# Attention and experts in one kernel: mark steps split, small planes moved between engines, block 0's queries turned by DMA, new issue sequences

## The chip, the cores and the metric

The kernel runs on one core of a Trainium2 chip. The metric is the device time of one execution in microseconds; of the kernel before there are three, 710.06, 710.90 and 711.39 us. TensorE (PE) does matmuls, VectorE (DVE) and ScalarE (ACT) read PSUM and SBUF, GpSimd (POOL) reads only what others have put into SBUF, and SyncE (SP) issues nearly all DMAs.

## The reference

For each of 4 batches, a key/value image of 384 x 32 x 128 is averaged over 4 x 4 windows to 768 rows and multiplied by `w_sr`; the result is both keys and values of an attention over 12288 queries of width 128. Its 49152 output rows go through a mixture of 8 experts: the gate's largest logit names one expert, whose two layers (128 to 1024 with a ReLU, 1024 to 128) are applied and scaled by the gate's probability.

```python
kv_flat = kv.reshape(B, H//4, 4, W//4, 4, C).mean(axis=(2, 4)).reshape(B, -1, C) @ w_sr
a = softmax(q @ kv_flat.T / sqrt(C));  x = a @ kv_flat          # B x 12288 x 128
e = argmax(x @ w_gate);  g = softmax(x @ w_gate)[e]
out = g * (relu(x @ w1[e]) @ w2[e])                             # per token
```

## The kernel before

**Tiles and stages.** The 49152 queries are cut into 96 blocks of 512, 24 to a batch. `keys(b)` loads and pools a batch's keys (12 loads of 512 KB; for batch 0 the last four come as 8 halves), multiplies them by `w_sr` and makes from them the scaled keys KT, the values v16 and the square M. `expert(b)` guesses the expert that the batch's tokens will choose from the mean value (`guess`, L837), loads that expert's `raw` weights, and sorts and packs its 1024 hidden units into 384 places (the side on which each unit lies, L945; keys, classes, the permutation PU, L1052; w1U and w2U). `block(t)` then does one block: queries in halves of fp16 turned to qT; scores s by two matmuls for each of three pairs of key tiles; ACT's exponential e; DVE's difference r (L1285); po from r, qT, v16 and M; halves xp of po, turned to x; three hidden tiles ph on w1U; and py on L and w2U, scaled to y and stored.

**Marks.** Tokens whose expert is not the guessed one, or that are not sure, are marked in `code`; `marks` (L1470) does so for 24 blocks at a time, for the last batch in two parts. Its steps go to and fro between DVE and POOL. One of them, `quiet` (L1518), needs flags that PE sums (`seen`, L1512) when all hidden tiles of those blocks are done. Lists of marked tokens are then counted (L1536 or L1543, L1810 to 1813), and a loop at the end (L1855) redoes what is listed.

**The order of the work.** Every operation is declared by `op(engine, duration, function, time, needs, gives, buffers)`. ORDER holds for each engine the sequence in which its operations are issued; a number is an operation's place among those that the code declares for that engine. WAYS names the choices that are taken where an operation is declared in two ways (`way=(name, 0 or 1)`): with the name in WAYS the second holds, without it the first. Names are for example `q3` for the cast of block 3, `l5` for reading block 5's logits by DVE (else ACT), `x7` for splitting block 7's po by ACT and POOL (else ACT and DVE). The engines issue in order: an instruction that waits holds up all behind it on its engine, and SP's DMAs likewise. A planner with durations merges the sequences; it puts filler matmuls (`fill`, L1846) on PE where its own time line has a hole before 110 us or after 690 us. After a DVE operation with `lock=True` it makes the next POOL instruction wait for that one.

**Turning queries.** For `t < TURNED` (L1250, blocks 0 and 1) PE transposes the f32 queries, ACT copies them to fp16 and DVE subtracts (L1259). For the others POOL casts (L1263) and subtracts (L1265), and SP issues a transposing DMA (L1267).

## Time and profile before

| | us |
|---|---|
| three runs | 710.06, 710.90, 711.39 |
| the profiled execution | 711.34 |
| its span, first to last instruction | 709.5 |
| PE, DVE, ACT, POOL busy in it | 687.5, 623.9, 606.5, 533.3 |
| TensorE's granted clock, mean | 0.998 |

A busy share is an average over the span. The start (keys and the first expert) and the end have other limits than the 80 or so blocks between, and are looked at by themselves in the rows below. In a row of a timeline the first two numbers are start and duration in us, `[1.2 <-X]` is idle time before it and what ended it, and `x3` a count.

### The profile page before, as it was taken

The numbers are of one execution on the slowest core, as the hardware profiler recorded it, in microseconds if no ns is written. First come the engines' busy times: TensorE is split into PE (matmuls) and PEld (weight loads), VectorE is DVE, ScalarE is ACT, GpSimd is POOL, SyncE is SP. The second block draws the span as 40 slices with busy tenths as digits, with TensorE's granted clock in tenths as the row PEclk, the third lists the DMA queues.
The fourth block names the chain that finished last, engine by engine and source line by source line (L and its number), as shares of the span: only waits on it lengthen the run. The fifth ranks groups of instructions, "written<-read, shape, count | busy, mean of one in ns | idle before, by whom it ended". The sixth has DMA issues, their size and how long they took to land.

```text
span 709.5 us, 20719 instructions
## 1 busy us (share of the span) xinstructions
PE 687.5 (97%) x7853; PEld 542.0 (76%) x7853; DVE 623.9 (88%) x1279; ACT 606.5 (85%) x1128; POOL 533.3 (75%) x768
## 2 busy tenths in 40 slices
...
GB/s 334 216 252 131 234 260 196 150 214 202 207 238 239 220 236 201 178 205 200 202 221 223 247 226 262 124 206 221 178 204 108 200 126 184 234 150 124 164 67 101
DMA packets 325253, 139.84 MB, mean 197 GB/s; under 512 B 210668, under 2 KB 316270, under 8 KB 325152
## 3 DMA queue, kind: packets, MB, share of 16 engines
...
HBM read 60.69 MB, written 26.90 MB: 123 GB/s over the span
## 4 chain that ended last, share of the span: by engine, by line
PE 75%; DVE 9%; ACT 6%; DMA 5%; issue 3%; POOL 2%; SPq 0%; ACTq 0%; POOLq 0%; DVEq 0%
PE b L487 32%; PE po L487 23%; PE s L487 18%; DVE r L1285 4%; ACT e L1282 3%; DMA x<-xp 2%; DMA qT<-qp 2%; DVE xp L1326 1%; DMA kv<-in_kv_dram 1%; DVE y L1426 1%; ACT g L1391 1%; ACT b L1391 1%; ACT xp L1325 1%; POOL g L1387 0%; POOL g L1385 0%
## 5 line engine op out<-in xcount | busy, mean ns | idle before, releaser
L1285 DVE SCALAR_TENSOR_TENSOR r<-s,e 128x1024 bf16<-128x1024 f32 x288 | 347.3, 1216 | 29.6 <-ACT e L1282 26.8
L1282 ACT ACTIVATE e<-s 128x1024 f32<-128x1024 f32 x288 | 294.2, 1030 | 30.5 <-PE s L487 27.8
L487 PE MATMUL po<-v,r 128*128 128x144 f16 x2304 | 249.6, 226 | 0.9 <-DVE xp L1326 0.5
L487 PEld LDWEIGHTS <-r 128*128 128x128 bf16 x2304 | 167.5, 98 | 24.3 <-DVE xp L1326 3.1
L487 PE MATMUL s<-qT,KT 128*128 128x512 f16 x576 | 169.1, 379 | 4.6 <-DVE r L1285 2.6
L487 PE MATMUL b<-x,w1U 128*128 128x512 f16 x453 | 137.3, 379 | 1.3 <-DMA x<-xp 0.6
L487 PE MATMUL po<-M,qT 128*128 128x135 f16 x1152 | 132.0, 224 | 0.0
L1387 POOL TENSOR_TENSOR g<-X,g 80x512 f16<-80x512 f32 x94 | 108.7, 1156 | 25.5 <-ACT g L1391 14.3
L487 PE MATMUL b<-w2U,g 128*128 128x128 f16 x1104 | 121.8, 219 | 0.0
L487 PE MATMUL b<-L,x 128*128 128x128 f16 x1068 | 117.8, 219 | 0.1
L1265 POOL TENSOR_TENSOR qp<-qr,qp 128x512 f16<-128x512 f32 x94 | 108.6, 1158 | 11.8 <-DVE la L1004 2.6
L487 PEld LDWEIGHTS <-qT 128*128 128x128 f16 x1152 | 84.2, 98 | 27.8 <-issue 1.8
L487 PEld LDWEIGHTS <-x 128*128 128x128 f16 x1116 | 80.7, 98 | 16.8 <-issue 1.8
L1263 POOL CAST qp<-qr 128x512 f16<-128x512 f32 x94 | 57.3, 610 | 31.7 <-DMA qr<-in_q_dram 21.9
L487 PEld LDWEIGHTS <-g 128*128 128x128 f16 x1152 | 80.0, 98 | 0.2
L1385 POOL CAST g<-X 128x512 f16<-128x512 f32 x94 | 57.0, 610 | 28.3 <-ACT X L1383 7.0
L647 POOL TENSOR_TENSOR kv<-kv,kv 128x512 f32<-128x512 f32 x54 | 67.9, 1270 | 7.2 <-PE s L935 2.2
L487 PEld LDWEIGHTS <-KT 128*128 128x128 bf16 x576 | 50.5, 98 | 29.9 <-issue 8.3
L1391 ACT ACTIVATE g<-b,zb 128x512 f16<-128x512 f32 x96 | 66.5, 693 | 6.2 <-PE b L487 5.7
L1391 ACT ACTIVATE b<-b,zb 128x512 f32<-128x512 f32 x96 | 64.1, 668 | 8.3 <-PE b L487 7.9
L1426 DVE TENSOR_TENSOR y<-b,gt 128x512 f32<-128x512 f32 x92 | 62.8, 684 | 8.6 <-PE b L487 4.1
L487 PEld LDWEIGHTS <-w1U 128*128 128x128 f16 x480 | 45.1, 98 | 31.7 <-issue 1.1
...
## 6 DMA issues: line engine op xcount, KB each, us to landing
...
qT<-qp SPq DMA_TRANSPOSE x94, 3.9
```

Source lines behind the costliest of these rows:

```text
L487: return nc.tensor.matmul(o, l, r, start=start, stop=stop)
L647: nc.gpsimd.tensor_add(flat(to), flat(to), flat(of))
L1263: op("POOL", .62, lambda: nc.gpsimd.tensor_copy(qp.tile[:, 0], qr.tile), T - 1.9 * LEN, [("qr", t)], [("qh", t)], [qr, qp])
L1265: op("POOL", 1.17, lambda: nc.gpsimd.tensor_sub(qp.tile[:, 1], qr.tile, qp.tile[:, 0]), T - 1.8 * LEN, [("qh", t)], [("qp", t)], [qr, qp])
L1282: op("ACT", 1.03, lambda e=e, ps=ps: nc.scalar.activation(e.tile, ps.tile, AF.Exp), at + .6, [("s", t, s)], [("e", t, s)], [ps, e])
L1285: op("DVE", 1.22, lambda e=e, ps=ps, s=s: nc.vector.scalar_tensor_tensor(r.tile[:, 2 * s:2 * s + 2], ps.tile, 1.0, e.tile, op0=ALU.add, op ...
L1325: op("ACT", .59, lambda: nc.scalar.copy(xp.tile[:, 0], po.tile[:, :, :C]), A, [last], [("xh", t)], [po, xp], way=(xw, 0))
L1326: op("DVE", .69, lambda: nc.vector.tensor_tensor(xp.tile[:, 1], po.tile[:, :, :C], xp.tile[:, 0], op=ALU.subtract), A + .5, [("xh", t)], [ ...
L1385: op("POOL", .62, lambda: nc.gpsimd.tensor_copy(gg.tile[:, 0], gf.tile), at + 1.5, [("gf", t)], [("gh", t), ("g", t)], [gf, gg])
L1387: op("POOL", 1.16, lambda: nc.gpsimd.tensor_sub(gg.tile[:PAIRS, 1], gf.tile[:PAIRS], gg.tile[:PAIRS, 0]), at + 2, [("gf", t), ("gh", t), ( ...
L1391: op("ACT", .78, lambda u=u, ph=ph, zu=zu, to=to: nc.scalar.activation(to.tile[:, u] if to is gg else to.tile, ph.tile, AF.Relu, bias=zu() ...
L1426: nc.vector.tensor_tensor(y.tile[:, cs], py.tile.rearrange("p (c d) -> p c d", d=C)[:, cs], bc(gr["gt"].tile[:, 0, js], C)[:, cs], op=ALU. ...
```

## The change

- `TURNED` is the tuple `(1,)`: block 0's queries take the way by DMA.
- `EARLY` is 14 and now concerns casts of queries: with `q{t}` in WAYS, ACT does the cast (L1263) for that block, for t below 14. The choice for r (`r{t}{s}`) is kept for t below 10.
- `unit` (L697) loses one instruction, and `rest` uses its input.
- Four small steps of `expert` get a second way on POOL: `others` (of), the last two instructions of `sides` (sd), `limit` (tb), `bias` (zq). w1l gets a way by ACT and POOL (z), which WAYS does not take. w1s now also needs `mir`.
- In `marks`, `shift` is one instruction that needs only `whose`; a new POOL step `named` adds the constant behind `known`; `code` needs `named` and `quiet` and compares the flag itself. So `known` no longer needs the flags.
- WAYS and the five sequences are new. What they name is read off by counting operations.

The head of SP's sequence in names of what is given, before and after (kv.0.d.i is batch 0's load i of part d, kv.0.2.i.a a half of it; qr.t a block's queries, qTh.t its transposing DMA):

```text
before: kv.0.0.1 kv.0.0.0 kv.0.0.3 kv.0.0.2 kv.0.1.1 kv.0.1.0 kv.0.1.2 kv.0.1.3 kv.0.2.2.0 kv.0.2.3.0 kv.0.2.0.0 kv.0.2.1.0
        kv.0.2.1.1 kv.0.2.0.1 kv.0.2.3.1 kv.0.2.2.1 qr.1 qr.4 qr.2 qr.0 qr.6 qr.7 qr.5 qTh.4 qr.3 qTh.2 raw.0.1 raw.0.0
after:  kv.0.0.3 kv.0.2.1.1 kv.0.0.0 kv.0.0.1 kv.0.0.2 kv.0.1.1 kv.0.2.0.1 kv.0.1.0 kv.0.1.2 kv.0.1.3 kv.0.2.1.0 kv.0.2.2.0
        kv.0.2.3.0 kv.0.2.0.0 kv.0.2.2.1 kv.0.2.3.1 qr.0 qr.4 qr.1 qr.5 qr.2 qTh.0 qr.6 qr.3 qr.7 qTh.5 raw.0.1 qTh.4 raw.0.0
```

The end of DVE's sequence (ys is y, g.95 block 95's hidden tile, 3.92 the marks of blocks 92 to 95):

```text
before: own?.3.92 ys.93 lp.3.72 mk2.3.92 se.25 gf.95 gate.25 whose.3.92 ok.3.92 g.95 quiet.3.92 ys.92 ys.95 known.3.92 code.3.92 lp.3.92 rest left.3
after:  gf.95 lp.3.72 rs.25 whose.3.92 ys.93 se.25 g.95 known.3.92 quiet.3.92 gate.25 code.3.92 ys.92 lp.3.92 ys.95 rest left.3
```

ACT's sequence begins, with pT and vTd the two reads of a part of the keys:

```text
before: pT.0.0 vTd.0.0 pT.0.1 vTd.0.1 pT.0.2.0 vTd.0.2.0 pT.0.2.1 qTh.1 vTd.0.2.1 KT.0.2 KT.0.0 e.1.2 kt.0 qTh.0 v16.0 e.1.1
after:  pT.0.0 vTd.0.0 pT.0.1 vTd.0.1 qh.0 pT.0.2.0 qh.4 pT.0.2.1 vTd.0.2.0 vTd.0.2.1 qTh.1 KT.0.2 qh.5 e.1.2 up.1.1 e.1.1 kt.0 v16.0
```

The diff, with the sequences cut to the first line of each engine:

```diff
-PE 1 0 2 4 3 5-7 9 8 10 110 11-12 98 113 13-14 112 17 99 111 15 101 16 145 18-19 24 100 114 144 116-117 115 20 146 104-105
...
-ACT 0-6 114 7 9 8 117 10 105 12 116 106 11 115 13 108 22 15 14 139 21 16-17 107 138 118 140 109-110 123 122 24 142 141 124
...
-DVE 0 3 1 4 2 6-7 5 10 9 11 13-14 8 12 180 16 15 17 19 18 183 22 175 23 182 176 181 20 24 178 21 25 201 26 44 177 200 185
...
-POOL 247 111 133-134 118-119 0 137 1 145 138 141-142 146 122-123 8-11 2 4 3 5 162 13 12 163 14 154 15 158-159 155 6 127 179
...
+PE 0-2 9 3-7 10 8 11 109 12 112 13 111 17 14 110 15 98 100 16 144 18-19 24 99 115 143 116 113-114 20 145 104 101-103 154 122
...
+ACT 0-3 103 4 137 6 5 7 111 8 146 115 114 113 9-10 112 11 127 155 104 106 12-13 20 139 19 14-15 105 138 116 140 107 147 121
...
+DVE 0-1 3 2 4 13 6-7 5 10 9 11 14 8 12 15-17 19-20 18 24 177 25 21 26 176 22 27 170 23 175 172 195 28 45 171 179 194 178
...
+POOL 119 249 118 141 144 0-1 127 124 147 128 150 131 151 11 10 13 15 2 4-6 12 14 162 166 16 159 17 163 8 135 120 134 132-133
...
+SP 3 11 0-2 5 9 4 6-7 10 12 14 8 13 15 76 91 80 95 83 77 99 87 103 96 18 92 17 20 19 21-22 16 107 84 115 111 119 81 88 100
...
 WAYS = dict.fromkeys("""
-k0 k2 t00 t01 d0 t10 d1 t20 d2 t30 b3 d3 x0 l1 l2 x3 l9 l11 l14 l15 x19 l20 l21 l22 l28 l30 l35 l37 l38 l39 x41 l41 l43 x46
-l46 l49 x57 l59 x69 l70 x71 l72 l76 x77 x78 x79 x80 l81 x82 x83 l85 x86 l86 x87 l87 x88 l88 x91 l91 l93 l94
+k2 t01 sd0 tb0 d0 zq0 t10 sd1 d1 zq1 t20 d2 zq2 t30 b3 of3 sd3 tb3 d3 zq3 q0 x0 l0 r11 l1 l2 q3 x3 q4 q5 q6 l6 q8 l8 l9 q10
+q11 l11 q12 l12 l16 l18 x19 l20 l24 l25 l26 l27 l29 l34 l37 x41 l41 l42 l43 x46 l46 l53 x57 l59 l64 l68 x69 x71 l74 l75 l76
+x77 l77 x78 x79 x80 x83 l84 l85 l86 x87 x89 l89 l90 x91 l91 l92 l94 l95
 """.split(), 1)
...
-    TURNED = 2
+    TURNED = (1,)
...
-    EARLY = 10
+    EARLY = 14
...
-            nc.vector.tensor_scalar_mul(cn[:, 8:9], cn[:, 3:4], scale)
...
-            nc.gpsimd.tensor_scalar(cn[:, 9:10], cn[:, 8:9], XS, 0.0, op0=ALU.mult, op1=ALU.add)
+            nc.gpsimd.tensor_scalar(cn[:, 9:10], cn[:, 3:4], scale * XS, 0.0, op0=ALU.mult, op1=ALU.add)
...
-        op("DVE", .97, unit, at + 2, [("pd", b), ("mean", b)], [("unit", b)], [pd])
+        op("DVE", .84, unit, at + 2, [("pd", b), ("mean", b)], [("unit", b)], [pd])
...
-        cg = buf("cg", [P, 6, E])
+        cg = buf("cg", [P, 7, E])
...
-        op("DVE", .7, others, at + 12, [("cg", b)], [("off", b)], [cg], lock=True)
+        def others_too():
+            c = cg.tile
+            some = c[:, 6, :EO]
+            nc.gpsimd.tensor_scalar(some, c[:, 1, :EO], c[:, 0, EO:], 1.0, op0=ALU.mult, op1=ALU.mult)
+            nc.gpsimd.tensor_tensor(c[:, 0, :EO], c[:, 0, :EO], some, op=ALU.add)
+            nc.gpsimd.tensor_scalar(c[:, 4, 1:2], cn[:, 12:13], -1.0, -1.0, op0=ALU.mult, op1=ALU.add)
+            nc.gpsimd.tensor_scalar(some, c[:, 1, :EO], c[:, 4, 1:2], 1.0, op0=ALU.mult, op1=ALU.mult)
+            nc.gpsimd.tensor_tensor(c[:, 2, :EO], some, iota_e[:, :EO], op=ALU.add)
+
+        op("DVE", .7, others, at + 12, [("cg", b)], [("off", b)], [cg], lock=True, way=(f"of{b}", 0))
+        op("POOL", 1.05, others_too, at + 12, [("cg", b)], [("off", b)], [cg], way=(f"of{b}", 1))
...
-        op("DVE", .98, sides, at + 8.5, [("mw", b)], [("side", b)], [pm, pz, sg], lock=True)
+        def sides_read():
+            nc.vector.tensor_copy(col(0)[:, :2 * in2].rearrange("p (b i) -> p b i", b=2), pm6()[:, :, :, P])
+            nc.vector.tensor_copy(col(0)[:, 2 * in2:], pz2()[:, :, P])
+
+        op("DVE", .98, sides, at + 8.5, [("mw", b)], [("side", b)], [pm, pz, sg], lock=True, way=(f"sd{b}", 0))
+        op("DVE", .6, sides_read, at + 8.5, [("mw", b)], [("side", b)], [pm, pz, sg], lock=True, way=(f"sd{b}", 1))
...
-        op("POOL", .6, mirror, at + 9, [("side", b)], [("mir", b)], [sg])
+        def sides_mirror():
+            nc.gpsimd.tensor_scalar(col(1), col(0), 0.0, 1.0, op0=ALU.is_gt, op1=ALU.mult)
+            nc.gpsimd.tensor_scalar(col(2), col(1), -2.0, 1.0, op0=ALU.mult, op1=ALU.add)
+            mirror()
+
+        op("POOL", .6, mirror, at + 9, [("side", b)], [("mir", b)], [sg], way=(f"sd{b}", 0))
+        op("POOL", 1.0, sides_mirror, at + 9, [("side", b)], [("mir", b)], [sg], way=(f"sd{b}", 1))
...
-        op("DVE", .39, limit, at + 35, [("class", b), ("unit", b)], [("Tb", b)], [la], lock=True)
+        def limit_too():
+            nc.gpsimd.tensor_scalar(cn[:, 14:15], top(NC - 1), 0.97 / 2 * NK * NK, 0.5, op0=ALU.mult, op1=ALU.min)
+            nc.gpsimd.tensor_scalar(cn[:, 13:14], cn[:, 3:4], KEYS_MIN, cn[:, 14:15], op0=ALU.is_ge, op1=ALU.mult)
+
+        op("DVE", .39, limit, at + 35, [("class", b), ("unit", b)], [("Tb", b)], [la], lock=True, way=(f"tb{b}", 0))
+        op("POOL", .42, limit_too, at + 35, [("class", b), ("unit", b)], [("Tb", b)], [la], way=(f"tb{b}", 1))
...
-           [("wT", b), ("side", b)], [("w1s", b)], [wT, sg, w1s], lock=True, way=(f"d{b}", 0))
+           [("wT", b), ("side", b), ("mir", b)], [("w1s", b)], [wT, sg, w1s], lock=True, way=(f"d{b}", 0))
...
-           [("wT", b), ("side", b)], [("w1s", b)], [wT, sg, w1s], way=(f"d{b}", 1))
+           [("wT", b), ("side", b), ("mir", b)], [("w1s", b)], [wT, sg, w1s], way=(f"d{b}", 1))
...
+        op("ACT", 1.15, lambda: nc.scalar.activation(raw[0].tile, w1s.tile, AF.Copy, scale=ws.tile[:, 4:5]), at + 18.5,
+           [("w1s", b), ("ws", b), ("mw", b), ("pT2", b)], [("w1t", b)], [w1s, raw[0], ws], way=(f"z{b}", 1))
+        op("POOL", 1.92, lambda: nc.gpsimd.tensor_sub(w1l.tile, rows(raw[0].tile), w1h.tile), at + 19.5, [("w1h", b), ("w1t", b)],
+           [("w1l", b)], [raw[0], w1h, w1l], way=(f"z{b}", 1))
...
-           [("w1h", b), ("key", b)], [("w1l", b)], [w1s, w1h, w1l, ws], lock=True)
+           [("w1h", b), ("key", b)], [("w1l", b)], [w1s, w1h, w1l, ws], lock=True, way=(f"z{b}", 0))
...
-        op("DVE", .5, bias, at + 20, [("ws", b)], [("zp", b)], [w2e, sg], lock=True)
+        def bias_too():
+            z = w2e.tile
+            nc.gpsimd.tensor_copy(z[:, :, P], col(5))
+            nc.gpsimd.tensor_sub(z[:, :, P + 1], col(5), z[:, :, P])
+
+        op("DVE", .5, bias, at + 20, [("ws", b)], [("zp", b)], [w2e, sg], lock=True, way=(f"zq{b}", 0))
+        op("POOL", .42, bias_too, at + 20, [("ws", b)], [("zp", b)], [w2e, sg], way=(f"zq{b}", 1))
...
-        if t < TURNED:
+        if t in TURNED:
...
+            qway = f"q{t}" if t < EARLY else None
...
-               [qr, qp])
+               [qr, qp], way=(qway, 0) if qway else None)
+            if qway:
+                op("ACT", .59, lambda: nc.scalar.copy(qp.tile[:, 0], qr.tile), T - 1.9 * LEN, [("qr", t)], [("qh", t)],
+                   [qr, qp], way=(qway, 1))
...
-            way = f"r{t}{s}" if t < EARLY else None
+            way = f"r{t}{s}" if t < 10 else None
...
-        def shift():
-            nc.gpsimd.tensor_scalar(ex(), ex(), 1.0, known - unknown, op0=ALU.mult, op1=ALU.add)
-            nc.gpsimd.tensor_scalar(ok(), ok(), -1.0, 1.0, op0=ALU.mult, op1=ALU.add)
-
-        step("POOL", .4 + fixed(.16), shift, 5, ["whose", "ok", "quiet"], "shift", [mo])
+        step("POOL", .2 + fixed(.16), lambda: nc.gpsimd.tensor_scalar(ex(), ex(), 1.0, known - unknown, op0=ALU.mult, op1=ALU.add),
+             5, ["whose"], "shift", [mo])
...
+        step("POOL", .2 + fixed(.16), lambda: nc.gpsimd.tensor_scalar(ex(), ex(), 1.0, unknown, op0=ALU.mult, op1=ALU.add),
+             5.7, ["known"], "named", [mo])
...
-            code[:, cols], ex(), unknown, ok(), op0=ALU.add, op1=ALU.mult), 6, ["known"], "code", [mo], True)
+            code[:, cols], ok(), 0.5, ex(), op0=ALU.is_lt, op1=ALU.mult), 6, ["named", "quiet"], "code", [mo], True)
...
```

## Rows read from the trace of the kernel before

**Rows 1.** The page's first part, and two of its costliest groups of instructions.
```profile
PE 687.5 (97%) x7853; PEld 542.0 (76%) x7853; DVE 623.9 (88%) x1279; ACT 606.5 (85%) x1128; POOL 533.3 (75%) x768
...
L1285 DVE SCALAR_TENSOR_TENSOR r<-s,e 128x1024 bf16<-128x1024 f32 x288 | 347.3, 1216 | 29.6 <-ACT e L1282 26.8
...
L1265 POOL TENSOR_TENSOR qp<-qr,qp 128x512 f16<-128x512 f32 x94 | 108.6, 1158 | 11.8 <-DVE la L1004 2.6
```

**Rows 2.** Busy time of each engine by stretches: PE, PEld, DVE, ACT, POOL, clock, DMA.
```profile
25.00:42.00 17.00, 16.01 (x117) 10.53 (x118) 15.56 (x41) 14.50 (x23) 10.11 (x14) 1.00 0.92 271
42.00:75.00 33.00, 31.00 (x335) 24.63 (x334) 31.24 (x65) 25.60 (x40) 23.93 (x34) 1.00 0.75 171
...
85.00:704.00 619.00, 613.56 (x7185) 484.30 (x7183) 551.56 (x1090) 552.57 (x1036) 487.54 (x698) 1.00 0.93 193
...
80.00:90.00 10.00, 10.00 (x103) 6.88 (x101) 8.82 (x13) 9.99 (x21) 8.57 (x14) 1.00 1.11 207
```

**Rows 3.** Waits of PE: for whom, us in total, times, longest.
```profile
PE s L487 <- DVE wg_st L529: 8.1, 1, 8.1
PE s L487 <- DVE r L1285: 2.9, 10, 0.6
```

**Rows 4.** Filler matmuls up to 85 us: ns min/median/max, first and last start.
```profile
L487 PE MATMUL b<-slots x42: 322/326/327, 18.6 to 63.4; 128*128 128x384 f16 x42
```

**Rows 5.** Timeline of DVE, 26 to 70 us: start, duration, instruction.
```profile
26.14 0.35 DVE L732 TENSOR_SCALAR KT<-vT,con 128x256 bf16<-128x256 f32 x1
...
28.83 0.68 DVE L1259 TENSOR_TENSOR qT<-b,qT 128x512 f16<-128x512 f32 x1
...
30.45 0.15 DVE L842 TENSOR_SCALAR first<-con 128x1 int32<-128x1 f32 x1
...
46.03 0.18 DVE L948 TENSOR_SCALAR sg<-sg 128x8 f32<-128x8 f32 x1
...
69.55 0.31 DVE L1123 CAST w2e<-sg 128x8 f16<-128x8 f32 x1
...
69.99 1.92 DVE L1052 TENSOR_SCALAR PU<-slots,sg 128x384 f16<-128x384 f16 x8
```

**Rows 6.** Timeline of PE: last keys, turning the first weights, first matmul on w1U.
```profile
22.01 1.06 PE L487 MATMUL s<-ident,r 128*128 128x128 f32 x8
...
39.42 1.04 PE L935 MATMUL s<-ident,raw 128*128 128x128 f32 x8
...
75.48 0.38 PE L487 MATMUL b<-x,w1U 128*128 128x512 f16 x1
```

**Rows 7.** Timeline of POOL (first query cast) and of ACT (last key half).
```profile
22.17 0.61 POOL L1263 CAST qp<-qr 128x512 f16<-128x512 f32 x1 [20.12 <-DMA qr<-in_q_dram]
...
23.10 0.28 ACT L602 ACTIVATE pT<-s 128x128 f32<-128x128 f32 x1 [0.63 <-PE s L487]
```

**Rows 8.** SP's issues: query transposes, the first w1 load, landing of the raw loads.
```profile
L1267 SPq DMA_TRANSPOSE qT<-qp x6: 1232/1266/1979, 26.0 to 58.0; - x6
...
32.22 0.44 SPq L907 DMA_DIRECT2D raw<-in_moe_w_dram  x1
...
DMA to landing us min/median/max: 4.6/5.0/5.3
```

**Rows 9.** Timeline of DVE, the last 8 us of the span.
```profile
701.92 1.41 DVE L1426 TENSOR_TENSOR y<-s,gt 128x512 f32<-128x512 f32 x3
...
703.24 0.17 DVE L1527 SCALAR_TENSOR_TENSOR mo<-lg,mo 128x16 f32<-128x16 f32 x1
703.52 0.18 DVE L1529 SCALAR_TENSOR_TENSOR code<-mo 128x16 f32<-128x16 f32 x1
...
705.30 0.21 DVE L1813 TENSOR_SCALAR n_left<-more,before 128x1 int32<-128x1 f32 x1
```

**Rows 10.** The chain that ended last near 270 us, and that stretch's busy time.
```profile
267.14 7.72 DMA qT<-qp
...
270.00:275.00 5.00, 3.98 (x63) 3.67 (x62) 4.90 (x11) 3.76 (x8) 4.79 (x6) 1.00 1.17 272
```

241 lines of the change are left out of this document (123 added, 118 removed), and 18 rows, old and new, of the table ORDER.

## Prediction, made before the result was known

> **What bounds the kernel now.** I read the page's first line and its costliest groups, then the busy time by stretches, PE's waits and PE's filler, and for the parts of the change the timelines of the first 76 us and of the last 10, where the chain of waits runs.
>
> PE is busy for 687.5 of 709.5 us [rows 1]. The stretches show where the other 22 us lie: 3.0 between 25 and 75 us, 5.4 in the whole 619 us after 85 [rows 2], 8.1 before its first matmul [rows 3], and the rest in the loading of the keys and at the end. Where PE waits after that start, it waits most for DVE's r: 2.9 us in 10 waits [rows 3]. Its busy time holds filler as well, matmuls on slots16 that nobody reads: 42 of 54 run between 18.6 and 63.4 us, and all 54 have 0.326 us each, which overlap by about half as all of PE's do; at half that the 42 are 6.8 us [rows 4]. From 25 to 75 us, then, PE has some 9.5 us to spare (3.0 idle and most of the filler), and a later start of real work costs what it takes. From 85 us on there is next to nothing to spare: the end is the moment at which PE's useful queue is full, plus the work left, plus 5.4, plus the tail.
>
> What holds that moment up is seen in DVE's timeline. In 25 to 75 us DVE is busy for 46.8 of 50 us [rows 2], and the chain hops through it: unit, the first subtraction r (L1285), block 0's qT, guess (L838 to 842), which releases the weight load, then sides, then the permutation PU, and only then the expert's matmuls [rows 5]. The first matmul on w1U, with which PE's backlog starts, comes at 75.48 [rows 6].
>
> **The change, part by part.** I worked out what each changed number of the sequences stands for by counting the operations in the order in which the code lists them.
>
> *Key loads.* The two loads for the first addition now stand third and fourth on SP, behind 768 KB. So the first addition starts later; all bytes together are the same, and the last of them land as before. PE's additions of one half of the last rows move ahead, which takes up to one group of 8 (1.06 us) out from behind the last load [rows 6]: a gain of 1.0 at most. Against it stand, besides PE's later start, ACT's q casts of blocks 0 and 4, now ahead of its reads of the last two halves. The second q load was there only at 22.17, when POOL began on it with a cast of 0.61; ACT read the last half at 23.10 [rows 7]. With q 4 at 22.17, a cast like POOL's 0.61 and the other read (0.28 and more) about that, ACT is again at 23.1; with the q loads 1 us later it is at 24.1. The ends are -1.0 and +1.0. I take 0, which is where the row of the q load puts it.
>
> *Block 0 not turned on PE.* PE loses 4 transposes, in a stretch where it has filler: nothing. ACT loses one copy; DVE loses the subtraction at 28.83, which takes 0.68 just ahead of guess, whose last instruction begins at 30.45 [rows 5]. That is -0.7. In its place stand an ACT cast, a POOL subtraction and a transposing DMA. Block 1's subtraction moves behind guess.
>
> *unit* drops one instruction of one element a partition; the nearest is guess's last, 0.15, and those overlap: -0.1. *KT's* first slice goes from ACT to DVE (as the other, 0.35) ahead of unit [rows 5], while block 0's maxima move ahead of mean, where DVE has been waiting: +0.1. Guess's last instruction then begins 0.7 earlier, at 29.75.
>
> *SP.* The w2 load is the first to follow guess, but a transposing DMA (block 4's q) is now between it and the w1 load. A transposing issue holds SP for 1.27 us, a plain one for 0.44 [rows 8]. Before, w1 left 1.77 after guess's last instruction, at 32.22; now 29.75 + 1.77 + 1.27 is 32.8, and with at most 5.3 to land [rows 8] and the 0.44 of issue 38.5. PE began to turn the weights at 39.42 [rows 6], so there are 0.9 us of cover, and with all else 0.7 earlier still 0.2. This costs nothing; without the cover up to +0.8. [...]
>
> *DVE from guess to the permutation.* Out go one r of block 1 (now an ACT copy and a POOL subtraction), two instructions of sides (0.18 each, overlapping: -0.3) and bias (0.44 from 69.55 to the permutation at 69.99) [rows 5]. In come one kt slice (0.35, as KT's), block 1's qT (0.68) and one read of logits (64 columns against qT's 512; an estimate from that is 0.2). The page has r at 1.216 [rows 1]. Net -1.2 + 0.35 + 0.7 + 0.2 - 0.3 - 0.45 = -0.7. The moved limit comes after the permutation. The POOL subtraction, 128x1024 from two f32 tiles, has no row; two of the 128x512 ones are 2.3 us (1.158 each) [rows 1]. Its result is needed only at 42 us, when DVE is done with block 1's other parts: covered, and up to 2.3 if it weren't. What covers the casts is ACT's idle time, 9.9 us of the 50 from 25 to 75 [rows 2]. ACT's queue gets a copy of about the length of e (1.03) and seven casts of about 0.6 there, and loses three of 0.4 to 0.6 and some reads: net some 3 us. If half of it lay on the path it would cost 1.5. I take 0, since the idle time is three times the load.
>
> Start in all: -0.7 - 0.7 = -1.4, with ends from +1.1 (casts 1.5 and key loads 1.0 more) to -3.0 (the key loads' 1.0 on top, and DVE's waits for ACT shorter by as much as half a microsecond).
>
> *Mark steps.* Until the last block these are off the path: DVE and POOL have room. At the end the chain runs over them [rows 9]: DVE has read the flags (quiet) when it begins three y at 701.92, which take 1.41, then come known (703.24) and code (703.52), two list steps, PE's count and four instructions, the last from 705.30 to 705.51. In the new order known stands ahead of the flags; behind them stand one reciprocal, code, block 92's y (half of the 1.41), the list steps, the last y and the count's instructions. So code begins near 702.2; the 2.0 from there to the end, and 1.4 for the two y less 0.3, which DVE waited for the count before, make 705.3. That is -0.2; at most -0.9 (both y after the end of the chain, with no output late), at least 0. The 4 us after that to the span's end stay.
>
> *The sequences after 85 us.* PE's 5.4 us of gaps are single waits; 1.0 stands in 270 to 275 us alone, where a transposing DMA of 7.7 us is in the chain [rows 10]. Nothing in the rows says that a new order has more or less of them: 0, with ends -3 and +4.
>
> Sum: -1.4 - 0.2 = -1.6. The profiled execution took 711.34, so it would take 709.7; that execution stands 0.44 above the median of 710.9, so against the median 709.3.
>
> **Rivals.**
> 1. *The full gain.* The key loads give their 1.0, and ACT and POOL hide everything, so PE's 9.5 us shrink by 3.0; the tail gives 0.9. For it: ACT's idle time. Against it: the q casts behind late q loads. 710.9 - 3.9 = 707.0.
> 2. *It comes earlier and is given back.* From 80 us on ACT and POOL are full as well (9.99 of 10 in 80 to 90) [rows 2]; if PE's backlog then lives from ACT, what comes earlier waits for it. Left are the tail and some tenths: 710.6. Against it: PE had no gap there, so there is backlog.
> 3. *Slower: late transposes.* One mechanism, in the stretches where the next batch's keys and weights are loaded (one for each of batches 1 to 3): SP issues transposes among the loads, they take 7 us and more, and PE, which has no spare work there, stands. Before, the slice from 270 to 275 us alone paid 1.0 [rows 10]. The new order adds one transpose and moves all loads. If all three stretches pay 1.0 in one slice and 0.6 around it, that is 4.8 against 1.6 before: +3.2, less the 1.6 gained: 712.5. It decides from 1.6 us of added waits on. Against it: all gaps after 85 us together are 5.4 now.
>
> **How the numbers follow.** Forecast 709.3, own range 708.0 to 710.2, chance 0.50; full gain 0.14; given back 0.17; slower 0.19. About 0.2%, 1.4 us, is what a measurement can tell from no change. Below 709.5 lie some 0.36 of the forecast's 0.50 and the full gain: faster 0.50. The rest of the forecast and rival 2 make 0.31 the same; slower 0.19. The range goes half way into the slow case and into most of the full gain: 706.8 to 712.3.
>
> **What would show it.** Right: guess's last instruction at about 29.75 instead of 30.45, the first w1U matmul near 74 instead of 75.48, fewer than 42 early fillers, code ahead of the last y and the last DVE step about 1.6 us before its old place; PE's gaps after 85 us again near 5. Wrong: ACT waiting for q loads ahead of the last key halves, so that the first scores come after 25.8; PE waits on qT or x of several us after 85; or guess earlier and w1U not.

## The result and the profile after

The changed kernel takes 714.33 us (median of 20 executions, 710.85 to 718.72), the kernel before 710.69 (20 executions, 708.86 to 711.7): ratio 1.0058, 95% interval [1.0043, 1.0072]. It is slower by 3.6 us where 1.6 less was forecast, and 714.33 lies outside the range of 706.8 to 712.3. The spread is wider as well: 8 us from the fastest to the slowest execution, against 3. (In the later sessions the kernel before spread over 3.5 to 5.3 us, and nine executions of the changed one over 3.3, so how much wider it is stays open.)

The execution profiled first took 717.91 us, at the upper end of that spread; two more were profiled later, at 714.90 (near the median) and 711.85. In the page of the first, PE's busy time has hardly changed, and POOL's subtractions of the queries now wait 39.2 us, 24.4 of them for ACT's casts, against 11.8 for anything at all [rows 1]:

```profile
PE 685.8 (96%) x7831; PEld 541.6 (76%) x7831; DVE 624.2 (87%) x1264; ACT 610.8 (85%) x1127; POOL 534.8 (75%) x781
...
L1305 POOL TENSOR_TENSOR qp<-qr,qp 128x512 f16<-128x512 f32 x95 | 109.7, 1161 | 39.2 <-ACT qp L1303 24.4
```

The same stretches as in [rows 2] (PE first, then PEld, DVE, ACT, POOL, the granted clock): from 25 to 42 us PE has lost 2.2 us and ACT has gained 1.0; after 85 us PE's gaps are 9.5 us instead of 5.4.

```profile
25.00:42.00 17.00, 13.85 (x99) 8.98 (x97) 14.13 (x39) 15.50 (x28) 11.06 (x14) 1.00 0.94 235
...
85.00:704.00 619.00, 609.49 (x7107) 481.47 (x7106) 549.61 (x1063) 551.40 (x1023) 485.40 (x701) 1.00 0.90 192
```

PE's waits, to be read beside [rows 3]: it has its first keys 2.6 us later (8.1 then; 6.5 and 3.6 now, with two tiny matmuls between), and a weight load stops it for 3.5 us, which no row of before has.

```profile
PE b L488 <- DVE wg_st L530: 6.5, 1, 6.5
PE s L488 <- DVE wg_st L491: 3.6, 1, 3.6
PE s L945 <- DMA raw<-in_moe_w_dram: 3.5, 1, 3.5
```

PE's timeline (start, duration), answering to [rows 6]. The last key group starts at 23.84 instead of 22.01, the first scores at 28.00 instead of 25.80, the turn of the weights at 40.66 instead of 39.42, the first matmul on w1U at 78.41 instead of 75.48:

```profile
10.73 6.22 PE L488 MATMUL s<-ident,kv 128*128 128x128 f32 x32 [3.65 <-DVE wg_st L491]
...
23.84 1.06 PE L488 MATMUL s<-ident,r 128*128 128x128 f32 x8
...
28.00 0.61 PE L488 MATMUL s<-qT,KT 128*128 128x512 f16 x2
...
40.66 1.04 PE L945 MATMUL s<-ident,raw 128*128 128x128 f32 x8
...
78.41 0.38 PE L488 MATMUL b<-x,w1U 128*128 128x512 f16 x1
```

On DVE, guess's last instruction starts at 31.96 and the permutation at 71.72, against 30.45 and 69.99 [rows 5]. SP issues the w1 load at 35.38 instead of 32.22 [rows 8], behind a transposing DMA:

```profile
31.96 0.15 DVE L842 TENSOR_SCALAR first<-con 128x1 int32<-128x1 f32 x1
...
71.72 1.93 DVE L1073 TENSOR_SCALAR PU<-slots,sg 128x384 f16<-128x384 f16 x8
```
```profile
33.81 1.31 SPq L1307 DMA_TRANSPOSE qT<-qp  x1
35.38 0.37 SPq L917 DMA_DIRECT2D raw<-in_moe_w_dram  x1
```

**Where the 3.6 us are.** The execution at 714.90 stands for the median. Cut both profiles at the end of PE's last useful matmul (702.48 before, 706.97 after) and read PE's busy time in four stretches, first before, then after:

```profile
0.00:25.00 25.00, 16.29 (x108) 15.02 (x109) 15.29 (x64) 4.77 (x14) 3.75 (x14) 1.00 0.86 300
25.00:50.00 25.00, 24.01 (x210) 17.49 (x211) 23.02 (x54) 18.97 (x30) 17.26 (x26) 1.00 0.86 249
50.00:85.00 35.00, 33.01 (x352) 24.86 (x350) 32.91 (x67) 30.17 (x51) 24.73 (x32) 1.00 0.88 172
85.00:702.48 617.48, 612.04 (x7176) 483.36 (x7174) 550.17 (x1085) 552.57 (x1036) 487.54 (x698) 1.00 0.94 193
```
```profile
0.00:25.00 25.00, 14.81 (x102) 13.73 (x102) 14.53 (x61) 4.86 (x14) 2.99 (x13) 1.00 0.86 297
25.00:50.00 25.00, 21.61 (x188) 15.61 (x188) 20.60 (x53) 19.69 (x30) 16.77 (x23) 1.00 1.01 245
50.00:85.00 35.00, 33.04 (x351) 24.85 (x351) 33.54 (x63) 32.02 (x53) 26.50 (x36) 1.00 0.85 186
85.00:706.97 621.97, 613.75 (x7189) 484.76 (x7186) 553.41 (x1081) 553.74 (x1032) 488.21 (x712) 1.00 0.91 192
```

Stretch minus busy is idle time. Up to 85 us it is 11.7 before and 15.5 after; 42 fillers with 8.8 us of busy time have become 33 with 7.2. Idle and filler together are 2.2 more; the useful rest of PE's busy time over the whole span, worked out as what is left, is 0.5 less, so the start counts for 1.7. After 85 us idle time is 5.4 and 8.2. From the last useful matmul to the end of the span it is 7.0 and 6.2. Start +1.7, stops after 85 us +2.8, tail -0.8: +3.7, the difference of the two spans (713.1 and 709.5). These are figures of one execution: in the other two profiles of the changed kernel the idle time after 85 us is 6.2 and 9.5.

### The profile page after: what moved, and what is told of

The parts are those of the page before. It is cut to its first block, busy times and chain, and to the rows that moved or that the text cites. A ratio compares the mean times of both kernels' runs of the same rounds, so it can differ in the third digit from the quotient of the medians.

```text
span 716.1 us, 20661 instructions
## 1 busy us (share of the span) xinstructions
PE 685.8 (96%) x7831; PEld 541.6 (76%) x7831; DVE 624.2 (87%) x1264; ACT 610.8 (85%) x1127; POOL 534.8 (75%) x781
## 3 DMA queue, kind: packets, MB, share of 16 engines
q8 instruction: 62, 1.02, 0.6%
## 4 chain that ended last, share of the span: by engine, by line
PE 74%; DVE 11%; DMA 5%; ACT 4%; POOL 2%; issue 2%; SPq 0%; POOLq 0%; ACTq 0%; DVEq 0%
PE b L488 33%; PE po L488 23%; PE s L488 17%; DVE r L1325 5%; ACT e L1322 2%; DMA qT<-qp 2%; DMA raw<-in_moe_w_dram 1%; DMA x<-xp 1%; DVE y L1466 1%; DMA kv<-in_kv_dram 1%; DVE xp L1366 1%; POOL qp L1305 1%; ACT xp L1365 1%; PE s L945 0%; ACT X L1423 0%
## 5 line engine op out<-in xcount | busy, mean ns | idle before, releaser
L488 PE MATMUL b<-x,w1U 128*128 128x512 f16 x453 | 139.6, 379 | 3.0 <-DMA x<-xp 1.2
L1305 POOL TENSOR_TENSOR qp<-qr,qp 128x512 f16<-128x512 f32 x95 | 109.7, 1161 | 39.2 <-ACT qp L1303 24.4
L1423 ACT ACTIVATE X<-b,zb 128x512 f32<-128x512 f32 x92 | 63.5, 695 | 4.9 <-PE b L488 4.5
```

Of the source, the lines that this page charges most:

```text
L488: return nc.tensor.matmul(o, l, r, start=start, stop=stop)
L1305: op("POOL", 1.17, lambda: nc.gpsimd.tensor_sub(qp.tile[:, 1], qr.tile, qp.tile[:, 0]), T - 1.8 * LEN, [("qh", t)], [("qp", t)], [qr, qp])
L1423: op("ACT", .69, lambda ph=ph, zu=zu: nc.scalar.activation(gf.tile, ph.tile, AF.Relu, bias=zu()), at + .5, [("ph", t, u), ("zb", b)], [("g ...
```

## The experiments

Times are medians, each ratio against the kernel before in the same session (710.69 to 711.3 us). "First scores" is their start on PE; "idle" is PE's idle time from 85 us to its last useful matmul; "low" is what was lost to the lower granted clock up to there (one minus the clock, summed over 1-us slices). The last four columns are of the profiled execution, the first of which is its time. Diffs of sequences show the changed stretch alone.

| kernel | median | ratio [95%] | profiled | first scores | idle | low |
|---|---|---|---|---|---|---|
| before | 710.69 | | 711.34 | 25.80 | 5.4 | 0 |
| changed | 714.33 | 1.0058 [1.0043, 1.0072] | 717.91 | 28.00 | 9.5 | 1.7 |
| after_again | 711.85, one | none | 711.85 | 27.10 | 6.2 | 0 |
| after_rep | 714.82 | 1.0047 [1.0031, 1.0063] | 714.90 | 27.32 | 8.2 | 0 |
| a_keys | 711.29 | 1.0011 [0.9998, 1.0025] | 710.23 | 26.41 | 5.3 | 0 |
| a_keys_rep | 712.26 | 1.0011 [0.9998, 1.0023] | 715.14 | 27.14 | 7.5 | 1.7 |
| b_keys | 714.47 | 1.0051 [1.0036, 1.0067] | 713.80 | 27.75 | 5.5 | 0 |
| a_first | 712.71 | 1.0024 [1.0007, 1.0042] | 711.70 | 26.28 | 5.0 | 1.7 |
| a_warm | 714.49 | 1.0044 [1.0027, 1.0061] | 714.41 | 28.30 | 7.1 | 0 |
| a_keys_warm | 712.33 | 1.0018 [1.0007, 1.0029] | 713.44 | 26.61 | 7.9 | 0 |
| a_warm2 | 713.90 | 1.0039 [1.0024, 1.0053] | 718.67 | 26.29 | 11.8 | 1.7 |
| a_keys_casts | 717.08 | 1.0083 [1.0063, 1.0103] | 717.55 | 26.43 | 7.9 | 1.7 |
| a_keys_pool | 713.18 | 1.0028 [1.0015, 1.0041] | 712.25 | 26.50 | 6.5 | 0 |
| b_tail | 711.68 | 1.0014 [1.0001, 1.0028] | 711.24 | 25.53 | 5.2 | 0 |
| a_w1 | 714.03 | 1.0035 [1.0021, 1.0049] | 714.85 | 27.95 | 8.3 | 0 |
| a_keys_m | 714.32 | 1.0046 [1.0031, 1.0062] | 711.82 | 27.13 | 5.7 | 0 |
| a_keys_sp | 711.72 | 1.0007 [0.9990, 1.0024] | 710.80 | 26.28 | 5.6 | 0 |
| b_late_w1 | 717.45 | 1.0080 [1.0063, 1.0098] | 717.93 | 25.80 | 10.1 | 1.7 |

### The order of the key loads

The first 16 issues of SP are the key loads; the other lines are PE's and VectorE's first steps on them. a_keys puts the old heads into the changed kernel, b_keys the new ones into the kernel before (its index 110 is 109 here):

```diff
-PE 0-2 9 3-7 10 8 11 109
+PE 1 0 2 4 3 5-7 9 8 10 109 11
-DVE 0-1 3 2 4 13 6-7 5 10 9 11 14 8 12
+DVE 0 3 1 4 2 6-7 5 10 9 11 13-14 8 12
-SP 3 11 0-2 5 9 4 6-7 10 12 14 8 13 15
+SP 1 0 3 2 5 4 6-7 12 14 8 10-11 9 15 13
```

a_keys. 

> The changed kernel with the 16 key loads of the first batch, and the first orders of TensorE and VectorE on them, put back as before; all else as changed. Theory A (the late start of the keys is the cost): the first key matmuls were 2.6 us later and the first scores 2.2 us later in the changed kernel (28.00 against 25.80). Put back, the first scores come at 25.8 or a little later (ScalarE's q casts may hold them by up to 0.5), guess's last instruction near 29.8, the first w1U matmul near 75.5, and the median falls by 2 to 3 us from 714.3, to 711.3 to 712.3. Rival B (TensorE's stops after 85 us, for late weight and transposed loads, are the cost): the start comes earlier, but the time stays within 0.7 of 714.3, and the stop of some 3.5 us on a weight load near 485 us is there again.

a_keys_rep. 

> a_keys again, in the same call as the changed kernel. Theory A: about 3 us less than it, as before (711.3). Rival: a_keys_m, which differs from a_keys by one step, had 714.3, so what a kernel gets depends on which stops it meets; then a_keys lies only 1 to 1.7 us below the changed kernel, as its first scores do (26.4 against 27.1 to 28.0).

b_keys. 

> The kernel before with the changed kernel's order of the 16 key loads of the first batch on SyncE, and of TensorE's and VectorE's first steps on them; all else as before. Theory A: the first key matmuls near 10.7 instead of 8.1, the first scores near 28 instead of 25.8, and a time 2 to 3 us above the kernel before (ratio 1.003 to 1.004). Rival B: the later start is taken up by TensorE's filler, of which there is some 9 us up to 75 us, and the time stays within 0.7 us of the kernel before.

In a_first only the two loads of the first addition go back to the front:

```diff
-SP 3 11 0-2 5 9 4 6-7 10 12 14 8 13 15
+SP 0-1 3 11 2 5 9 4 6-7 10 12 14 8 13 15
```

a_first. 

> The changed kernel with only the two loads of the first addition put first on SyncE, where they stood before; all other loads, TensorE's and VectorE's orders as changed. Theory A in its narrow form (it is the first addition's place alone): the addition starts near 6.8 instead of 9.36, the first key matmuls near 8.1 instead of 10.73, the first scores come 1.5 to 2.2 us earlier than 28.00, and the median falls by 1.5 to 3 us from 714.3. Rival: the other key loads, which the changed order still brings late, hold TensorE instead, and the first scores stay after 27.

Undone, the new order gives back 3.0 us of the median (714.33 to 711.29) and 2.6 when repeated (714.82 to 712.26); done alone it costs 3.6. PE's timelines of b_keys and of a_first:

```profile
10.43 5.33 PE L485 MATMUL s<-ident,kv 128*128 128x128 f32 x32 [3.35 <-DVE wg_st L488]
...
27.75 0.60 PE L485 MATMUL s<-qT,KT 128*128 128x512 f16 x2 [0.22 <-ACT KT L733]
```
```profile
8.07 3.75 PE L486 MATMUL s<-ident,kv 128*128 128x128 f32 x16 [0.99 <-DVE wg_st L489]
...
26.28 0.60 PE L486 MATMUL s<-qT,KT 128*128 128x512 f16 x2
```

The place of the first addition's loads is enough to move the first scores, here to 26.28 from 27.10, 27.32 and 28.00 in three profiles of the changed kernel; the median falls by 1.6. Theory A holds in sign and place. a_keys's guess comes at 30.37, the forecast for a_keys was 29.8, and its first w1U matmul at 76.82, not 75.5.

### Why PE couldn't make it up: its slow beginning

Groups of matmuls by form (count, busy us, mean ns), of the changed kernel from 10 to 15 us and from 16 to 18 us: 428 ns become 275. The kernel before has 434 ns from 8 to 13 us and 275 from 14 to 16.

```profile
L488 PE MATMUL s<-ident,kv 128*128 128x128 f32 x20 | 4.6, 428 | 3.6 <-DVE wg_st L491 3.6
```
```profile
L488 PE MATMUL s<-ident,kv 128*128 128x128 f32 x9 | 1.2, 276 | 0.0
```

The slow beginning moved with the first matmul, and after 10.73 us PE has hardly a gap until 24.9 in which to catch up (0.1 us, and three fillers).

How long it lasts differs between executions, and the first scores follow. In the three profiles of the changed kernel (changed, after_rep, after_again) 22, 17 and 12 matmuls up to 20 us took 421 ns or more, and the first scores came at 28.00, 27.32 and 27.10. In a_keys_rep, a_keys and a_keys_sp, with the old key loads, it is 23, 15 and 12 matmuls, and 27.14, 26.41 and 26.28. With like numbers side by side, then, the old key loads bring the first scores forward by 0.8 to 0.9 us in the changed kernel. In the old kernel it is 2.2 (b_keys with 13 slow ones, 27.75; b_tail with 15, 25.53).

If it belongs to PE's first microseconds of work, filler ahead of the keys takes it away:

```diff
-    plan.filler, plan.filler_times = (bank().make, fill, .487), ((8.5, 110.0), (690.0, 800.0))
+    plan.filler, plan.filler_times = (bank().make, fill, .487), ((3.0, 110.0), (690.0, 800.0))
```

a_warm. 

> The changed kernel, with TensorE's filler (matmuls whose result nobody reads) allowed from 3.0 us on instead of 8.5, so that TensorE is at work before the first keys are there; all else as changed. Theory C: the late first addition costs so much because TensorE's first 5 us of work are slow (its 128x128 f32 matmuls on the keys take 421 to 437 ns until 15.4 us and 275 ns after that; 32 of them took 6.22 us from 10.73), and that stretch moved with it. With filler ahead the 32 take about 3.9 us, the first scores come near 26 instead of 28.00, and the median falls by 1.5 to 2.5 us from 714.3. Rival: the loads that come last set the pace; the first scores stay at 27.5 or later and the time within 0.5 of 714.3.

a_keys_warm. 

> As a_keys (key loads in the order of before), and TensorE's filler from 3.0 us on. By theory C the first 16 key matmuls take 2.0 us instead of 3.71, but here the third addition waits for its load until 14.43 in any case, so only part is left: first scores 0.3 to 1.0 us earlier than 26.41, time 0 to 1 us below a_keys' 711.3. Rival: nothing, since the loads decide.

In a_warm2 the first four fillers have 5, 5, 10 and 10 matmuls instead of 3, so that they last until the keys come:

```diff
+    early = [5, 5, 10, 10]
+
     def fill(b):
-        for _ in range(3):
+        for _ in range(early.pop(0) if early else 3):
```

a_warm2. 

> The changed kernel with filler on TensorE from 2.7 us to about 10.6 without a long stop (in a_warm the filler stopped at 9.29, and the key matmuls from 11.10 were slow again at 421 to 443 ns). Theory C, tried properly: the first 32 key matmuls then take 275 to 285 ns each, 4 us or what their loads allow, instead of 6.2; TensorE waits for loads between them; first scores near 26 to 26.6 instead of 28.00, median 1 to 2 us below 714.3. Rival: the loads decide, first scores at 27.5 or later, median within 0.5 of 714.3.

PE's timelines of a_warm, a_keys_warm and a_warm2, in this order:

```profile
11.10 6.15 PE L486 MATMUL s<-ident,kv 128*128 128x128 f32 x32 [1.80 <-DVE wg_st L489]
```
```profile
8.03 2.02 PE L486 MATMUL s<-ident,kv 128*128 128x128 f32 x16 [1.55 <-DVE wg_st L528]
```
```profile
10.26 3.79 PE L486 MATMUL s<-ident,kv 128*128 128x128 f32 x32
...
26.29 0.61 PE L486 MATMUL s<-qT,KT 128*128 128x512 f16 x2
```

a_warm did not test it: its filler paused twice for 1.8 us, and the 32 were slow again, 6.15 us. In a_warm2 they take 3.79 us, and the first scores come at 26.29 although the loads are still in the late order, against 27.10 to 28.00; 0.4 to 0.6 of that is a first addition that was earlier in this execution (matmuls from 10.26). So the slow beginning is a good part of what the late addition cost up to the first scores. The median fell by 0.4 only, which is the rival's figure; the profiled execution, the slowest of the twelve, was stopped at 162, 410 and 491 us (2.40, 2.36 and 1.68 us). In a_keys_warm, with the old loads, the faster matmuls wait for loads, and nothing is gained (26.61 against 26.41).

### ScalarE's casts

In a_keys_casts ACT's casts of blocks 0 and 4 (103, 137) go behind the reads of the last key halves:

```diff
-ACT 0-3 103 4 137 6 5 7
+ACT 0-4 6 5 7 103 137
```

a_keys_casts. 

> As a_keys, and ScalarE's q casts of blocks 0 and 4 moved behind its reads of the last two key halves. If the casts hold the keys, as one end of the forecast's range had it, the first scores come up to 1.0 us earlier than in a_keys and the time falls by up to 1. If TensorE's own transposes of the keys set that moment, the first scores stay within 0.2 us of a_keys, and the time within 0.5 (block 0's transposed q may then come later and cost a few tenths).

In a_keys_pool the casts of blocks 3, 5 and 6 are POOL's again (WAYS loses q3, q5 and q6), each ahead of its subtraction.

a_keys_pool. 

> As a_keys, and the q casts of blocks 3, 5 and 6 on GpSimd again, each right ahead of its subtraction, instead of on ScalarE. Theory D: what is left of the change's loss at the start comes through ScalarE: it is busy for 16.2 of the 17 us from 25 to 42 in a_keys (14.5 before), so e comes late and VectorE waits for it (0.66, 0.78 and 0.64 us at 42 to 49 us). With three casts less there ScalarE falls to about 14.5, those waits shrink, the first w1U matmul comes about 0.5 us before 76.82, and the time falls by 0.3 to 0.8 from a_keys. Rival: GpSimd then delivers the transposed q later, TensorE waits longer for it, and the time is the same or up to 1 us more.

a_keys_casts is 4.8 to 5.8 us above the two runs of a_keys, and the first scores don't move (26.43). That doesn't clear the casts. ACT's rows, first a_keys, then a_keys_casts:

```profile
20.73 0.62 ACT L1301 CAST qp<-qr 128x512 f16<-128x512 f32 x1 [0.79 <-DMA qr<-in_q_dram]
21.25 0.27 ACT L601 ACTIVATE pT<-s 128x128 f32<-128x128 f32 x1
...
25.85 0.51 ACT L733 ACTIVATE KT<-vT,con 128x256 bf16<-128x256 f32 x1 [0.43 <-DVE con L688]
```
```profile
20.80 0.28 ACT L601 ACTIVATE pT<-s 128x128 f32<-128x128 f32 x1 [0.70 <-PE s L486]
...
24.34 1.14 ACT L1301 CAST qp<-qr 128x512 f16<-128x512 f32 x2
...
25.86 0.52 ACT L733 ACTIVATE KT<-vT,con 128x256 bf16<-128x256 f32 x1
```

In a_keys ACT waits for a q load with the cast of it, a key half is read behind that, and PE, with six fillers in between (21.27 to 22.41), begins the last key group at 22.47. With the casts moved the group begins at 21.66, and DVE has what KT needs at 25.34 instead of 25.82. But the casts now stand right ahead of KT, which starts when it did. So the casts hold the first scores at either place; a place behind KT was not tried.

Its transposed q of block 4 is late for PE, 2.44 us, and then PE runs at a granted clock of 0.72 from 39 to 41 us and of 0.50 from 41 to 43. PE's timeline and the stretches (PE's busy time first, the clock third from the end):

```profile
38.55 0.61 PE L486 MATMUL s<-qT,KT 128*128 128x512 f16 x2 [2.44 <-DMA qT<-qp]
```
```profile
37.00:39.00 2.00, 0.45 (x3) 0.31 (x4) 1.88 (x3) 1.26 (x4) 1.15 (x2) 1.00 1.10 303
39.00:41.00 2.00, 2.00 (x15) 2.00 (x14) 0.90 (x2) 1.71 (x2) 2.00 (x3) 0.72 1.04 404
41.00:43.00 2.00, 2.00 (x12) 2.00 (x12) 0.98 (x3) 0.67 (x4) 0.47 (x1) 0.50 1.05 367
```

a_keys_pool refutes theory D. ACT has its room back, 14.64 of 17 us against 16.19 in a_keys (first a_keys, then a_keys_pool), yet DVE's waits for ACT from 38 to 76 us are 3.2 us instead of 2.4, the first w1U matmul comes at 77.38 and the median is 713.18, no less than a_keys. PE's wait for block 4's q, which the rival had growing, is 0.62 us against 0.88.

```profile
25.00:42.00 17.00, 14.08 (x105) 9.42 (x106) 14.72 (x43) 16.19 (x26) 10.40 (x13) 1.00 0.91 244
```
```profile
25.00:42.00 17.00, 13.86 (x102) 9.06 (x103) 14.51 (x43) 14.64 (x24) 10.18 (x14) 1.00 0.99 259
```

### The mark steps alone

b_tail has the new steps in the last call alone, and at the end of VectorE's sequence known, quiet, code, one y, the list steps, the last y:

```diff
+        if lo < 92:
...
+        else:
+            step("POOL", .2 + fixed(.16), lambda: nc.gpsimd.tensor_scalar(ex(), ex(), 1.0, known - unknown, op0=ALU.mult, op1=ALU.add),
+                 5, ["whose"], "shift", [mo])
...
-DVE 868 861 870 811 862 871-875
+DVE 868 861 871 870 872 811 873 862 874-875
```

b_tail. 

> The kernel before with the new mark steps in the last call alone: known ahead of the flags, code by one comparison right behind them, and of the two last y one ahead of the list steps and one behind. Forecast: 0.2 us less (0 to 0.9). From the last mark of the flags to the last VectorE instruction it should be 3.5 us, as in the changed kernel's trace, instead of 3.76. If the y that now come later hold up the outputs instead, the time rises by up to 0.7.

No gain: ratio 1.0014 [1.0001, 1.0028]. From the mark of the flags (`quiet`) to the end of the last VectorE instruction it is 3.22 us (701.79 to 705.01) instead of 3.77, more than was expected. But `quiet` starts 1.15 us behind PE's count of the flags instead of 0.60, because `known` ahead of it waits for POOL:

```profile
701.69 0.18 DVE L1533 SCALAR_TENSOR_TENSOR mo<-lg,mo 128x16 f32<-128x16 f32 x1 [0.87 <-POOL mo L1531]
```

From PE's count of the flags to the start of the last VectorE instruction it is 700.64 to 704.85, 4.21 us, against 4.20 before (701.23 to 705.43). Then the span lasts 4.6 us longer, against 4.0 before: the last issues of stores on SP and ACT end 0.3 and 0.2 us ahead of that instruction, where it was 1.3 and 1.7. In the changed kernel PE also counts the flags two output groups earlier, 2.6 us before the end of its last useful matmul (704.38 and 706.97 in after_rep) instead of 1.25; by the rows it is this that shortens its tail by 0.8.

### Stops on late DMAs, and what follows them

In the first profile of the changed kernel the chain of waits goes through one load near 485 us (start, duration):

```profile
480.14 8.40 DMA raw<-in_moe_w_dram
488.54 0.14 issue
488.67 1.07 PE s L945 x8
```

The stretches behind it, and the matmuls there (ns min/median/max): 422 ns, where the kernel before has 276 for the same tiles.

```profile
486.00:488.67 2.67, 0.00 (x0) 0.03 (x1) 1.02 (x1) 0.10 (x1) 2.41 (x8) 1.00 0.50 55
488.67:490.00 1.33, 1.33 (x18) 1.20 (x19) 0.00 (x0) 0.00 (x0) 0.76 (x3) 1.00 0.79 176
490.00:492.00 2.00, 2.00 (x19) 2.00 (x16) 0.66 (x2) 1.95 (x4) 0.00 (x0) 0.56 1.19 301
492.00:494.00 2.00, 2.00 (x12) 1.91 (x11) 0.79 (x6) 1.37 (x4) 0.00 (x0) 0.59 0.93 248
```
```profile
L488 PE MATMUL s<-Ms,raw x12: 422/422/529, 490.4 to 492.9; 128*128 128x129 f32 x12
```

So this stop cost 3.50 us, and the granted clock behind it, 0.56 and 0.59, 1.7 more. b_late_w1 puts such a stop into the kernel before (72 is batch 3's w1 load):

```diff
-SP 301 69 72 376 73 362 347 328 351
+SP 301 69 376 73 362 347 72 328 351
```

b_late_w1. 

> The kernel before with one move: batch 3's w1 load on SyncE behind w2, a q load and a transposing load, some 5 us later. It should land near 489 and stop TensorE for 2 to 4 us at its turn of the weights (486.1), as in the changed kernel's first profile. Theory E: a stop that long is followed by some 3.5 us at the lower granted clock, which costs 1.7 more, so the median rises by the stop plus 1.7, 3.7 to 5.7 us above 711. Rival: the stop alone, 2 to 4 us.

PE's wait, and two stretches behind it:

```profile
PE s L485 <- DMA raw<-in_moe_w_dram: 4.0, 1, 4.0
```
```profile
490.00:492.00 2.00, 2.00 (x12) 2.00 (x11) 0.16 (x1) 0.54 (x2) 0.00 (x0) 0.54 1.15 265
492.00:494.00 2.00, 2.00 (x13) 1.98 (x12) 0.51 (x4) 0.00 (x0) 0.55 (x3) 0.60 1.01 237
```

4.0 and 1.7 make 5.7; the median rose by 6.15 (711.3 to 717.45), above the top of theory E's range by 0.45 and of the rival's by 2.15. The loss behind the stop is there.

In the changed kernel batch 3's w2 load stands ahead of w1; a_w1 swaps them as before. a_keys_m moves one DVE step behind M of batch 2; a_keys_sp is a_keys with the same swap and block 16's x (141) ahead of three stores and two q loads:

```diff
-SP 306 73 72 369
+SP 306 72 73 369
...
-DVE 451 448 442 103 100 455
+DVE 451 448 103 100 442 455
...
-SP 156 33 114 177 118 201 110 141 181
+SP 156 33 141 114 177 118 201 110 181
```

a_w1. 

> The changed kernel with batch 3's two weight loads on SyncE in the order of before (w1 ahead of w2); all else as changed. Theory B: in the profiled execution of the changed kernel w1 left 0.66 us behind w2, landed 8.4 us later and stopped TensorE for 3.5 us; its cover, from issue to the turn of the weights, was 5.0 us against 7.3 before. With w1 first the cover is 0.7 longer and it lands in 4 to 5 us: no stop, the median 0.5 to 2 us below 714.3 and the highest of the runs below 717. Rival: the stop was rare, and the median stays within 0.4 of 714.3.

a_keys_m. 

> As a_keys, with one step moved on VectorE: the gate sum (se) of group 9, which waits 0.54 us for ScalarE, goes behind M of batch 2 instead of ahead of the two steps that make it. Every profile of the changed kernel's sequences has one stop of 1.0 us near 315 us, TensorE waiting for that M; no profile of the sequences of before has it. If that stop is a cost of the new sequences like any other, it shrinks to 0.5 or less and the median falls by about 0.5 to 1 from a_keys' 711.3. Rival: there is slack behind it, and the time stays within 0.3.

after_again, the changed kernel unchanged. 

> The changed kernel once more, for a second profile. By theory B in its wider form, the new sequences keep TensorE's start where it was (first scores 28.0, first w1U matmul 78.4, both within 0.4), while the stops on late transposes and weight loads after 85 us differ from one execution to the next: 1 to 4 us in two to four places of 160 to 165, 350 to 355 and 485 to 491 us, and the 1.0 us near 317 again.

after_rep, the same. 

> The changed kernel again, timed beside a_keys again. The first two profiles of it differ by 6.0 us of span; 3.5 us of that is the stop on batch 3's w1 load at 485 us, and some 1.7 more is work at a granted clock of 0.5 to 0.62 from 490 to 494, which the other profile has not. If that is the usual source of the spread, this profile lies on the same line: its span is about 710 plus its stops on DMAs after 85 us beyond 1.7 us, plus 1.7 where one of them is followed by a low clock. Median 713.5 to 715.

a_keys_sp. 

> As a_keys, with two moves on SyncE: block 16's x ahead of two output stores and two q loads (it was late by 0.7 to 2.4 us at 162 us in five profiles), and batch 3's w1 load ahead of w2. Theory B: the stops at 162 and 486 us are gone, and the median is 0.5 to 1.5 us below a_keys of the same call. Rival: the stops move to other transposes on the same queue (as in a_w1, where qT and x stood in w1's place), and the median stays within 0.4.

PE's stops over 0.6 us after 85 us, by their end. Three profiles of the old sequences (before, b_tail, b_keys): at 275 to 278 (q, 1.00, 1.06 and 1.54) and 283 (x, 0.64 and 0.69). Fourteen of the new ones: near 317 in all (M; 0.83 in a_keys_m, else 1.02 to 1.05); near 162 in seven (x, 0.72 to 2.40); near 352 in four (x, 1.09 to 1.57); at 485 to 491 in seven (w1 0.94 to 3.50, in a_w1 q, 1.49); single ones elsewhere. The fourteen have 7.3 us of idle time after 85 on average, 5.0 to 11.8; the three have 5.2 to 5.5.

- a_w1's stop on w1 is gone, q and x stand in its place, and the median is 0.3 lower: the rival's number, though no execution took over 714.95 us.
- a_keys_m's stop shrank to 0.83 only, and its median, 714.32, is 2 to 3 us above a_keys's two: refuted, and why it is so much slower is open; its profile is that of its fastest execution (711.82).
- after_again and after_rep: first scores at 27.10 and 27.32, not within 0.4 of 28.00, so the start varies as well, with the slow beginning. after_again had 1.24 us at 351 and 0.53 at 406, less than expected. after_rep waited 3.8 us for DMAs after 85, for which the line gives a span of 712.1; it was 713.1.
- a_keys_sp has no stop at 162, 352 or 486, and lies 0.5 below a_keys_rep, the lower end of what was expected and too little to be told from nothing. It is the best version with the change, and not faster than the kernel before (1.0007 [0.9990, 1.0024]).

The profile of a_keys_rep, one of its slowest executions, shows the same pair elsewhere, a stop of 1.99 us on x and a granted clock of 0.52 behind it:

```profile
162.85 0.60 PE L486 MATMUL b<-x,w1U 128*128 128x512 f16 x2 [1.99 <-DMA x<-xp]
```
```profile
164.00:166.00 2.00, 2.00 (x12) 2.00 (x11) 0.84 (x3) 2.00 (x3) 1.82 (x5) 0.52 1.22 301
```

## Why the prediction was wrong, step by step

- *What bounds the kernel*: right. The end followed PE's idle time and filler, and the difference could be put together from them; only the early filler, taken at 6.8 us, is 8.8 of busy time.
- *Key loads, taken at 0 (-1.0 to +1.0)*: this step failed first. It said: "the first addition starts later; all bytes together are the same, and the last of them land as before". True of the bytes (the last key load lands at 20.23 before, at 19.73 in the changed kernel), but PE, not the last load, set the end of the keys: it worked without a gap from its first matmul on, at 428 ns a matmul at first. So of the 2.6 us at its start 2.2 went through to the first scores (1.3 and 1.5 in the other two profiles); the new order alone in the old kernel costs 3.6 us of time. The sign of error that the prediction named, first scores after 25.8, is what came, but it was sought in ACT's casts. In the changed kernel they don't hold the keys: ACT reads the last half 1.09 us after PE begins it (23.84, 24.93), as before (22.01, 23.10). With the old key loads they do, by the rows of a_keys and a_keys_casts, which is how a_keys's first scores can still be 0.6 later than before.
- *Block 0's qT off DVE, -0.7*: right. From the first scores to guess's last instruction it is 3.96 us (28.00 to 31.96) instead of 4.65.
- *SP, w1 behind a transpose, no cost*: right for the turn of the weights (39.02 in a_keys), though w1 left at 34.09 there and not at 32.8. What was left out is the transposed q on the same queue: PE waited about 1 us for block 4's (0.88 in a_keys), and in a_first and a_keys_casts, with waits of 1.27 and 2.44, a granted clock of 0.50 from 40 to 42 us followed.
- *DVE from guess to the permutation, -0.7*: failed. It is 39.76 us (31.96 to 71.72) against 39.54. The work did go off DVE, but on that way DVE waits longer for ACT (3.2 us instead of 1.4), which the prediction had free for the casts on the strength of an average over 50 us. a_keys_pool shows that ACT's load is not all of it.
- *Mark steps, -0.2*: right in sign and wrong in cause. The steps alone gain nothing; with PE's count of the flags earlier the tail is 0.8 shorter, near the far end of its range.
- *The sequences after 85 us, taken at 0 (-3 to +4)*: the second step that failed, and the larger term: +2.8 in the execution near the median, +0.8 and +4.1 in the other two. The new sequences leave less time between some loads and their use: batch 3's w1 load has 5.0 us from its issue to its turn instead of 7.3. "Nothing in the rows says that a new order has more or less of them" was so, but it was a reason for a wide range, not for 0 in a forecast of 1.6.
- *Rivals*: the slower one was the right kind, transposes and loads of the next batch's stretches, priced at +3.2 for stops of 1 us each. It missed that a stop can be paid again in clock, as the one of 3.50 us was with 1.7, and it did not have the key loads. The sum by terms as measured: start +1.7 instead of -1.4, sequences +2.8 instead of 0, tail -0.8 instead of -0.2.

Open: how the 2.6 to 3.0 us come about that a_keys gives back. With the slow beginning alike, its first scores are 0.8 to 0.9 us earlier. The rest seems to lie after 85 us: PE's idle time there is 8.5 us on average in the six profiles of the new sequences with the first addition's loads late (6.2 to 11.8), and 6.4 in the eight with them in front (5.0 to 7.9). Why a later start should meet more stops was not tried, and one profile of most kernels can't show how often it does.
